# One order of steps for another: a delta-rule attention with a gated feed-forward, its hand-written step list rearranged

## The chip, the core and the metric

The kernel runs on one core of one Trainium2 chip. The time is the device time of one launch in microseconds, from start to end as the device counts it; three runs of the kernel before gave a median of 515.95 us. The change is called faster or slower by the ratio of such times.

## What is computed

The reference has two halves. The first walks 768 tokens one after another for 4 batches x 8 heads, with a 48 x 48 state for each; the second is a gated feed-forward on its output (`x`, 4 x 768 x 384).

```python
k_n = k / (norm(k) + 1e-06)
for t in range(768):                       # (b, h): 4 x 8 states of 48 x 48
    y[:, :, t] = q_t @ state
    v_old = k_t @ state
    state = state + beta_t * outer(k_t, v_t - v_old)
x = y.transpose(0, 2, 1, 3).reshape(4, 768, 384)

h = gelu(x @ w_in)                         # 384 -> 1024
u, v = h[..., :512], h[..., 512:]
v_n = layer_norm(v) * g_ln
v_s = einsum('ts,bsd->btd', w_sg, v_n) + b_sg[None, :, None]
out = x + (u * v_s) @ w_out
```

## The kernel before

**Chunks and segments.** The walk over tokens is cut into chunks. The program counts 12 chunks, 0 to 11: each holds 64 tokens of two batches at once (16 pairs of batch and head, of which half lies on partitions 0 to 63 and half on 64 to 127), and chunks 0 to 5 serve one pair of batches and 6 to 11 the other. Two chunks are a segment (0 to 5). Within a chunk the recurrence is solved with matrices: the products of the chunk's keys and queries (`gram`), the inverse of a unit triangular matrix of 64 x 64 for each pair (its blocks of 32 x 32 on VectorE in `lanes`, the rest by small matmuls), and then a chain of matmuls that carries the state.

**Steps.** A string, PROGRAM, lists some 800 steps by name. A loop at the end of the function calls each in turn, so the string sets the order of instructions on every engine and in every queue. A step reads `name:chunk` or `name:half:chunk`; a letter names the queue of a DMA (S is SyncE's, A is ScalarE's, P is GpSimd's). Those that matter here:

- `kd:c:x:q`, `kq:c:x:q`, `kt`, `v`: loads of a chunk's keys and queries (448 KB each piece), by the helper `load` (L172). `kd` feeds `gram`, `kq` the chain. There are two buffers of each, so chunk 9's `kd` needs `gram:7` to be over. Each load further waits for the latest copy that a chain step before it in the list has marked (`own`'s or `state`'s copy on ScalarE).
- `gram:c` (matmuls `ps<-kd`), copied by ScalarE to `gm`; `gstore:c` (L267) writes a part of `gm` to DRAM (`gd`), `zload:s` (L342) reads a whole segment back as `zl`, in a layout that has the matrices along the partitions.
- `lanes:0`, or `bglanes:g` and then `l:n`: the inverse on `zl`. `bglanes` puts its operations (one or two for each column of a block; 58 or more for a group) into a list and `l:n` issues the next n of them, most on VectorE; the first makes a copy on VectorE (L364) and two `affine_select` on GpSimd (L366). Groups are segments 0, 1, 2 with 3, and 4 with 5. Its end stores `zd` (L470).
- `blocks:c` and `heads:c` (L476): the stored inverse comes back as `z` and `zk`. They issue whatever is left of the segment's `l` operations first.
- `turned`, `join:0..3` (chunks 0 to 3), `corner_a`, `corner_b`: matmuls with a masked copy on VectorE between them (`j`, L504), which put the blocks of 64 x 64 together.
- `old:e:c`, `own:e:c`, `state:e:c` for e = 0, 1: the chain. `old`'s product is added to `v` on VectorE (L616), `own`'s is copied to `u` (L638), `state`'s to `s` and `x` (L651, L666) on ScalarE. `old:1` may carry a third argument, the chunk whose first quarter of `gram` it is mixed with.
- `turn:c` (L767), `gate:c:d` (L745 to L747), `values:c:n` (L781): the feed-forward's first layer for a chunk that is through the chain, in pieces. `ustore`, `xstore`, and a store within `values` go through SyncE's queue. `d:n` decodes a piece of `w_in` on VectorE and ScalarE, `w:k` loads one, `norms`, `mask`, `vprep` are small preparations.
- `kick`, `warm`: matmuls on zeros that nobody reads. `unit`, `late_weights`, `last_part`: decoding of the late weights.

What comes behind the list (the spatial product with `w_sg` and the last projection, 864 matmuls, "the tail" below) is ordered by the compiler and is the same in both kernels.

TensorE has one helper line, L115, for nearly all matmuls of the attention, so rows are told apart by their tiles: `ps<-kd` is `gram`, `ps<-j,ztk` is `join` or `corner_b`, `ps<-s,kq` is `old`, `ps<-v,z` is `own`.

Of the kernel before, what the change touches and what calls it, by code (L numbers as in the profile page):

```python
# [67 lines left out]
l:2 corner_a:6 kt:6:S turned:6 gate:4:1 gate:4:2 gate:4:3 own:1:5 l:1 vprep:6 corner_b:6 l:3 state:1:5 l:9 kq:7:0:S
turn:5 old:0:6 heads:7:P kt:7:P own:0:6 state:0:6 values:4:8 l:13 old:1:6 kq:7:1:S values:4:10 blocks:7:S gate:5:0
v:7:S vprep:7 values:5:16 ustore:4 gate:5:1 l:1 values:5:2 mask:10 l:1 turned:7 xstore:5 corner_a:7 l:2 own:1:6 l:1  # L70
state:1:6 turn:6 gate:5:2 gate:5:3 bgnorm l:2 ustore:5 old:0:7 values:6:5 corner_b:7 kq:8:1:P xstore:6 blocks:8:S:P
kq:8:0:A norms:4 v:8:A own:0:7 gate:6:0 heads:8:S:P values:6:4 state:0:7 old:1:7 vprep:8 own:1:7 gate:6:1 values:6:2
gate:6:2 turned:8 heads:9:A state:1:7 blocks:9:A corner_a:8 kt:8:P gate:6:3 values:6:1 l:8 v:9:P values:6:4 turned:9
corner_b:8 old:0:8 turn:7 own:0:8 kq:9:0:P state:0:8 ustore:6 corner_a:9 l:11 norms:5 l:7 old:1:8 vprep:9 xstore:7
l:11 values:6:2 own:1:8 gate:7:0 state:1:8 corner_b:9 heads:10:S:P late_weights kq:9:1:S unit:1 gate:7:1 values:7:5
mask:9 old:0:9 kt:9:S unit:1 v:10:P values:7:13 kq:10:0:S own:0:9 turn:8 gate:7:2 values:8:1 gate:7:3 kt:10:S unit:1
blocks:10:A ustore:7 state:0:9 gate:8:0 gate:8:1 unit:1 old:1:9 turned:10 unit:1 gate:8:2 own:1:9 gate:8:3 kq:10:1:A
kq:11:0:A unit:1 ustore:8 corner_a:10 mask:11 state:1:9 turn:9 heads:11:A vprep:10 values:8:10 old:0:10 gate:9:0
corner_b:10 unit:1 gate:9:1 blocks:11:S own:0:10 values:8:5 unit:1 v:11:A xstore:8 state:0:10 unit:1 gate:9:2
kq:11:1:P unit:1 values:8:2 values:9:5 unit:1 old:1:10 vprep:11 corner_a:11 values:9:2 unit:1 turned:11 own:1:10  # L80
unit:1 values:9:11 state:1:10 unit:1 kt:11:A gate:9:3 turn:10 corner_b:11 old:0:11 unit:1 ustore:9 unit:1 unit:1
gate:10:0 values:10:14 own:0:11 xstore:9 values:10:4 unit:1 state:0:11 gate:10:1 old:1:11 own:1:11 gate:10:2
# [1089 lines left out]
```

## Time and profile before

| | us |
|---|---|
| median of three runs | 515.95 (514.07 to 516.02) |
| the profiled execution | 512.55 |
| its span in the trace | 510.8 |
| TensorE busy | 452.8 (89% of the span) |
| VectorE busy | 332.4 (65%) |
| ScalarE busy | 171.8 (34%) |
| mean granted clock of TensorE | 0.92 |

The span is what the trace covers; the profiled execution took 1.75 us more than that, and the median run 3.40 us more than the profiled one. The chain of work that ended last is 74% TensorE, 13% DMA, 7% VectorE and 3% ScalarE. A granted clock of 1.00 is 2.4 GHz, one of 0.50 is 1.2 GHz.

### The profile page before, as it was taken

How to read it: one execution, taken by the hardware profiler on the slowest of the kernel's cores; microseconds unless marked ns; L12 is line 12 of the kernel's file. 1: busy time of each engine (PE TensorE's matmuls, PEld its weight loads, DVE VectorE, ACT ScalarE, POOL GpSimd, SP SyncE). 2: the span in 40 equal slices, each digit the busy share in tenths (PEclk: the TensorE clock that was granted, in tenths of full speed). 3: DMA queues.
4: the chain of work that ended last, by engine and by line, in shares of the span. 5: the costliest groups of instructions: out<-in, count | busy, mean ns of one | idle time of the engine just before them, and what ended most of it. 6: DMA issues, size and time to landing. Idle time of an engine off the chain costs nothing.

```text
span 510.8 us, 17402 instructions
## 1 busy us (share of the span) xinstructions
PE 452.8 (89%) x7563; PEld 414.5 (81%) x7563; DVE 332.4 (65%) x728; ACT 171.8 (34%) x403; POOL 92.7 (18%) x120
## 2 busy tenths in 40 slices
...
PEclk9875765795999997899999999999999999999999
...
GB/s 203 213 271 220 152 239 150 130 174 246 110 166 283 262 187 196 198 111 214 196 188 200 279 222 226 232 121 224 280 176 151 170 155 116 101 154 149 85 17 139
DMA packets 96557, 93.30 MB, mean 183 GB/s; under 512 B 55184, under 2 KB 71552, under 8 KB 96480
## 3 DMA queue, kind: packets, MB, share of 16 engines
...
q14 instruction: 18, 0.15, 0.1%
...
## 4 chain that ended last, share of the span: by engine, by line
PE 74%; DMA 13%; DVE 7%; ACT 3%; issue 2%; SPq 1%; POOL 0%; ACTq 0%; POOLq 0%; DVEq 0%
PE ps L115 23%; PE ps L745 14%; PE ps L747 13%; PE ps L746 13%; PE ps L781 9%; DMA gd<-gm 3%; DMA zl<-gd 3%; DMA kd<-kqT 3%; DMA kq<-kqT 2%; PE ps L767 1%; DVE ztmp L420 1%; DVE zl L427 1%; SPq L267 1%; DMA z<-zd 1%; DMA v<-vtok 1%
## 5 line engine op out<-in xcount | busy, mean ns | idle before, releaser
L888 POOL TENSOR_TENSOR ga<-ga,uT 128x384 f32<-128x384 f32 x32 | 35.7, 1118 | 144.5 <-DMA vraw<-vD 54.0
L115 PE MATMUL ps<-s,kq 48*64 48x48 f32 x1408 | 54.4, 228 | 4.6 <-ACT s L651 3.5
L115 PEld LDWEIGHTS ps<-s,kq 48*64 48x64 f32 x1408 | 48.2, 142 | 11.7 <-issue 4.9
L115 PE MATMUL ps<-kd 48*64 48x128 f32 (+1 forms) x768 | 33.4, 350 | 22.9 <-DMA kd<-kqT 19.3
L115 PEld LDWEIGHTS ps<-kd 48*64 48x64 f32 x768 | 30.3, 191 | 24.2 <-issue 16.4
L745 PE MATMUL ps<-xh,winh 128*128 128x256 f32 x144 | 43.6, 303 | 0.0
L750 ACT CAST gh<-ga 128x384 fp32r<-128x384 f32 x32 | 16.3, 511 | 75.1 <-POOL ga L888 69.5
L746 PE MATMUL ps<-xl,winh 128*128 128x256 f32 x144 | 40.6, 282 | 0.0
L747 PE MATMUL ps<-xh,winl 128*128 128x256 f32 x144 | 40.6, 282 | 0.0
L115 PE MATMUL ps<-z,gm 32*64 32x64 f32 x640 | 27.5, 248 | 12.2 <-DMA z<-zd 11.8
L751 DVE TENSOR_TENSOR gl<-ga,gh 128x384 fp32r<-128x384 f32 x32 | 18.5, 580 | 29.7 <-ACT gh L750 29.6
L420 DVE TENSOR_TENSOR ztmp<-zl 128x28 f32<-128x28 f32 (+20 forms) x84 | 36.0, 428 | 2.7
L427 DVE TENSOR_TENSOR zl<-zl,ztmp 128x28 f32<-128x28 f32 (+20 forms) x84 | 35.9, 427 | 2.4
L115 PEld LDWEIGHTS ps<-z,gm 32*64 32x64 f32 x640 | 24.6, 158 | 14.9 <-issue 12.4
L115 PE MATMUL ps<-v,z 64*64 64x48 f32 x768 | 31.6, 231 | 5.4 <-DVE v L616 3.0
L115 PEld LDWEIGHTS ps<-v,z 64*64 64x64 f32 x768 | 27.9, 146 | 7.4 <-DVE v L616 2.7
L745 PE MATMUL ps<-wsgh,vnh 128*128 128x384 f32 x96 | 32.6, 340 | 0.0
L745 PE MATMUL ps<-wsgh,winh 128*128 128x384 f32 x96 | 32.5, 339 | 0.0
L746 PE MATMUL ps<-wsgl,winh 128*128 128x384 f32 x96 | 32.5, 339 | 0.0
L747 PE MATMUL ps<-wsgh,winl 128*128 128x384 f32 x96 | 32.5, 339 | 0.0
L747 PE MATMUL ps<-wouth,gl 128*128 128x384 f32 x96 | 32.4, 339 | 0.0
L745 PE MATMUL ps<-wouth,gh 128*128 128x384 f32 x96 | 32.3, 339 | 0.0
(140 smaller groups left out, 1141.4 us busy)
## 6 DMA issues: line engine op xcount, KB each, us to landing
...
kd<-kqT ACTq DMA_DIRECT2D x9, 448.0 KB, 5.9
```

Of the source, the lines that this page charges most:

```text
L115: return nc.tensor.matmul(out=out, lhsT=lhsT, rhs=rhs, start=start, stop=stop, skip_group_check=True)
L267: queues[(half + sd) % len(queues)].dma_start(out=gdt[s][half, sd, c2].rearrange("j s t -> s j t"), in_=GK[c % N_M][r0:r0 + 32, half],)
L420: tv.tensor_tensor(out=products(i, r0, r1, at), in0=zb[:, :, r0:r1, i:i + 1].broadcast_to([P, nblk, r1 - r0, w]), in1=zb[:, :, i:i + 1, i ...
L427: tv.tensor_tensor(out=z_, in0=z_, in1=products(i, r0, r1, at), op=ALU.add)
L745: nc.tensor.matmul(out=ps, lhsT=sh, rhs=mh, start=(first and i == 0), stop=False)
L746: nc.tensor.matmul(out=ps, lhsT=sh, rhs=ml, start=False, stop=False)
L747: nc.tensor.matmul(out=ps, lhsT=sl, rhs=mh, start=False, stop=(last and i == n - 1))
L750: nc.scalar.copy(out=hi, in_=src)
L751: nc.vector.tensor_tensor(out=lo, in0=src, in1=hi.bitcast(F32), op=ALU.subtract)
L767: nc.tensor.transpose(out=ps[:, cc], in_=x[:, cc * P:(cc + 1) * P], identity=ident)
L781: nc.tensor.matmul(out=self.ps, lhsT=(self.xl if k == 2 else self.xh)[:, cc, bi], rhs=(winl if k == 1 else winh)[:, cc, DH:], start=(i == ...
L888: nc.gpsimd.tensor_tensor(out=gv, in0=gv, in1=uT[:, :, d], op=ALU.mult)
```

## The change

The list has the same steps in another order, and with other letters for the queues. No matmul is added or removed: the 4587 matmuls, the 858 VectorE and all ScalarE instructions of the two programs are the same in number and shape. What differs is where they stand, how `l` operations and `values` matmuls are split among the steps, and which queue issues a DMA: SyncE's has 293 instead of 303 of them, ScalarE's 39 instead of 54, GpSimd's 93 instead of 68.

The core of the diff is the list's opening and the two stretches that the prediction speaks of:

```diff
-keys:1:S keys:0:A consts beta:A kq:1:0:P kq:1:1:S kgram:0 kgram:1 kd:3:1:S gstore:0:S:A gstore:1:P kd:3:0:P kq:0:0:S
-kick:12 zload:0:A kd:2:1:A l:1 kd:2:0:A qgram:1 lanes:0 gram:3 kd:5:0:P gram:2 warm:9 kq:0:1:P w:0:A kt:0:P
-gstore:2:S:P kd:4:1:A v:0:S d:1 kd:4:0:A norms:0 d:1 gstore:3:S:A:P mask:3 qgram:0 blocks:0:S:P mask:0 d:1 zload:1:A
-join:0:0 heads:0:S bglanes:1 turned:0 join:1:0 vprep:0 l:1 join:2:0 join:3:0 mask:1 corner_a:0 kt:1:A blocks:1:S:P
-heads:1:P kd:5:1:S l:1 gram:5 old:0:0 gram:4 w:2:P v:1:S l:2 corner_b:0 kd:6:0:P l:28 join:0:1 kd:6:1:P kd:7:0:P l:2
+kick:12 beta:P keys:0:A keys:1:A kq:1:0:P consts kgram:0 kq:1:1:P kd:2:1:P gstore:0:S:P l:3 kgram:1 gstore:1:S:A:P
+zload:0:S kd:3:0:S w:0:S kd:3:1:P lanes:0 kd:2:0:A gram:3 norms:0 kd:5:0:P kq:0:1:A qgram:1 kq:0:0:P mask:3 l:5 gram:2
+qgram:0 mask:0 kd:4:0:S kd:4:1:P l:1 warm:9 gstore:2:S:P gstore:3:P blocks:0:A d:1 l:2 heads:0:S:A mask:1 v:0:S d:2
+zload:1:S join:0:0 turned:0 bglanes:1 kt:1:S v:1:S join:1:0 join:2:0 vprep:0 kd:5:1:A l:3 old:0:0 join:3:0 corner_a:0
+blocks:1:P l:6 corner_b:0 l:29 gram:4 gram:5 kt:0:P join:0:1 w:1:P vprep:1 kd:6:1:P kd:7:0:P kd:7:1:P heads:1:S:A
...
-own:1:1 mask:4 join:3:2 turn:0 mask:2 v:2:S corner_a:2 state:1:1 d:1 blocks:3:S:P turn:1 join:0:3 gstore:7:S:A:P
-corner_b:2 d:2 join:1:3 heads:3:S kd:9:0:A kd:8:0:P zload:2:P turned:3 zload:3:S bglanes:2 gram:8 v:3:S d:1 l:1
-kq:2:1:A kd:9:1:S l:2 vprep:2 xstore:1 old:0:2 gram:9 kt:2:A join:2:3 kq:3:0:S own:0:2 l:3 kq:3:1:A l:1 kd:10:1:S l:22
+v:2:A gstore:7:S:P heads:3:S:P join:3:2 corner_a:2 old:1:1:8 zload:2:P own:1:1 zload:3:P blocks:3:S d:3 kd:9:0:S
+state:1:1 mask:2 bglanes:2 kt:2:S kd:9:1:P gram:8 l:4 kq:2:1:P vprep:2 corner_b:2 l:8 join:0:3 turn:1 gstore:8:S:P
+turned:3 old:0:2 join:1:3 l:6 gram:9 kd:10:0:P v:3:P own:0:2 norms:3 gate:0:0 l:7 vprep:3 l:8 kd:11:1:P join:2:3
...
-gstore:8:S:P gstore:9:S:P kd:11:1:P kq:5:1:P state:1:3 gate:1:2 gate:1:3 v:5:P ustore:1 gate:2:0 gram:11 gate:2:1
-blocks:4:S:P l:5 xstore:2 heads:4:S:A:P gate:2:2 gate:2:3 turn:3 values:2:16 mask:7 kt:5:S corner_a:4 gram:10 turned:4
-gstore:10:S mask:6 old:0:4 zload:4:S vprep:5 mask:8 gate:3:0 values:2:1 heads:5:S:P corner_b:4 norms:3 gstore:11:S
-own:0:4 ustore:2 mask:5 gate:3:1 state:0:4 blocks:5:S:P zload:5:P kq:5:0:A gate:3:2 gate:3:3 old:1:4 values:2:1
-own:1:4 turned:5 state:1:4 bglanes:3 l:14 corner_a:5 xstore:4 old:0:5 xstore:3 l:4 corner_b:5 heads:6:P turn:4
+own:1:3 gate:1:3 xstore:2 gate:2:0 ustore:1 blocks:4:S v:5:A norms:2 mask:8 state:1:3 kq:5:1:P gate:2:1 heads:4:S:P
+gram:10 turn:3 mask:6 gstore:10:S:P gate:2:2 vprep:4 zload:4:S mask:7 values:2:4 gram:11 values:2:7 gstore:11:S:A
+vprep:5 old:0:4 gate:2:3 values:2:3 turned:4 corner_a:4 gate:3:0 heads:5:S mask:5 corner_b:4 l:7 mask:10 ustore:2
+zload:5:P gate:3:1 kq:5:0:P own:0:4 blocks:5:P gate:3:2 bglanes:3 turned:5 state:0:4 old:1:4 values:2:3 l:13
+values:2:1 heads:6:S:A:P own:1:4 gate:3:3 l:3 v:6:P state:1:4 corner_a:5 turn:4 blocks:6:S:P l:3 turned:6 l:3 old:0:5
...
```

Three places of it, as the engines' queues have them. In the rows, `kd_95`, `kq_107` and `z_105` are the buffers of odd chunks, `kd_94`, `kq_106` and `z_104` those of even ones, and `gm_96` to `gm_103` those of chunks 8 to 11 and 4 to 7.

SyncE's queue before, from the blocks of chunk 3 on:

```order
L476 DMA z_105<-zd 32x16x32 x2
L267 DMA gd<-gm_103 32x16x32
L476 DMA zk<-zd 64x8x32 x4
L342 DMA zl<-gd 128x1024
L172 DMA v_110<-vtok 128x2x384
L172 DMA kd_95<-kqT 112x2x512
L812 DMA xD_73<-x 128x2x384
L172 DMA kq_107<-kqT 112x2x512
```

and after:

```order
L267 DMA gd<-gm_103 32x16x32 x2
L476 DMA zk<-zd 64x8x32 x2
L476 DMA z_105<-zd 32x16x32 x4
L172 DMA kd_95<-kqT 112x2x512
L172 DMA kt_113<-ktok 128x2x384
L267 DMA gd<-gm_96 32x16x32 x2
L172 DMA kq_107<-kqT 112x2x512
L788 DMA vD_75<-vg 128x512
```

The reload of segment 3 (`zl`, `zload:3`) has left SyncE's queue, and a piece of chunk 9's keys (`kd_95`) stands right behind the blocks of chunk 3. GpSimd's queue at the same place, before:

```order
L476 DMA z_105<-zd 32x16x32 x2
L267 DMA gd<-gm_103 32x16x32
L172 DMA kd_94<-kqT 112x2x512
L342 DMA zl<-gd 128x1024
L366 AFFINE_SELECT zl<-zl 128x1024 x2
L172 DMA kt_114<-ktok 128x2x384
```

and after:

```order
L267 DMA gd<-gm_103 32x16x32 x2
L476 DMA zk<-zd 64x8x32 x2
L342 DMA zl<-gd 128x1024 x2
L172 DMA kd_95<-kqT 112x2x512
L366 AFFINE_SELECT zl<-zl 128x1024 x2
L172 DMA kq_106<-kqT 112x2x512
```

Both reloads of the pair of segments, the other piece of chunk 9's keys and, behind the two selects, a piece of chunk 2's `kq` now stand in this queue. SyncE's queue some 70 us later, at the stores of chunks 10 (`gm_98`) and 11 (`gm_99`), before:

```order
L267 DMA gd<-gm_98 32x16x32 x4
L342 DMA zl<-gd 128x1024
L476 DMA zk<-zd 64x8x32
L267 DMA gd<-gm_99 32x16x32 x4
L807 DMA uD_77<-ut 128x2x512
L476 DMA z_105<-zd 32x16x32 x2
```

and after:

```order
L267 DMA gd<-gm_98 32x16x32 x2
L342 DMA zl<-gd 128x1024
L788 DMA vD_75<-vg 128x512
L267 DMA gd<-gm_99 32x16x32 x2
L476 DMA zk<-zd 64x8x32 x2
L807 DMA uD_77<-ut 128x2x512
```

Half of each chunk's four stores have gone to other queues. The reload `zl` between them is `zload:4`; `zload:5` is in GpSimd's queue in both kernels.

## Rows read from the trace of the kernel before

**Rows 1.** The page: busy time by engine, and TensorE's granted clock in 40 slices.

```profile
PE 452.8 (89%) x7563; PEld 414.5 (81%) x7563; DVE 332.4 (65%) x728; ACT 171.8 (34%) x403; POOL 92.7 (18%) x120
PEclk9875765795999997899999999999999999999999
```

**Rows 2.** Stretches: start:end length, busy (count) of each engine, granted clock, DMA share, GB/s.

```profile
68.40:95.70 27.30, 25.92 (x563) 24.05 (x565) 22.45 (x46) 10.68 (x31) 5.62 (x8) 0.50 0.60 153
96.00:113.00 17.00, 14.28 (x514) 12.96 (x506) 12.98 (x23) 8.14 (x20) 3.22 (x5) 1.00 0.75 186
116.20:129.80 13.60, 6.25 (x164) 5.89 (x168) 11.28 (x27) 4.36 (x15) 2.50 (x2) 0.50 0.73 233
198.10:208.30 10.20, 5.56 (x103) 4.97 (x104) 9.59 (x25) 2.23 (x5) 2.70 (x4) 0.50 0.38 88
209.00:350.00 141.00, 135.01 (x2861) 116.72 (x2860) 98.40 (x231) 58.34 (x136) 9.59 (x14) 1.00 0.69 201
354.00:510.00 156.00, 153.22 (x868) 152.71 (x867) 80.60 (x149) 34.08 (x60) 35.71 (x32) 1.00 0.48 145
```

**Rows 3.** Chain that ended last, 107 to 131 us: start, length, what.

```profile
107.42 6.39 DMA gd<-gm
113.93 0.35 SPq L342
114.37 0.40 SPq L172
114.82 8.49 DMA kd<-kqT
123.55 6.85 PE ps L115 x192
```

**Rows 4.** TensorE's timeline, 110 to 129 us; in brackets the idle time before.

```profile
110.84 1.98 PE L115 MATMUL ps<-kd 48*64 48x128 f32 x64
123.55 3.69 PE L115 MATMUL ps<-kd 48*64 48x128 f32 x64 [9.82 <-DMA kd<-kqT]
127.17 1.74 PE L115 MATMUL ps<-j,ztk 64*32 64x32 f32 x64
```

**Rows 5.** DMA issues of 0 to 140 us: queue, count, size, median us to landing.

```profile
kd<-kqT ACTq DMA_DIRECT2D x8, 448.0 KB, 5.9
kd<-kqT POOLq DMA_DIRECT2D x6, 448.0 KB, 4.6
kd<-kqT SPq DMA_DIRECT2D x5, 448.0 KB, 5.8
kq<-kqT POOLq DMA_DIRECT2D x2, 448.0 KB, 5.8
```

**Rows 6.** GpSimd's timeline, 117 us: the selects of `lanes`.

```profile
117.95 2.50 POOL L366 TENSOR_SCALAR_AFFINE_SELECT zl<-zl 128x1024 f32<-128x1024 f32 x2 [9.98 <-DVE d L364]
```

**Rows 7.** The stretch 100 to 150 us, columns as in rows 2.

```profile
100.00:150.00 50.00, 36.38 (x1037) 32.20 (x1037) 45.66 (x87) 18.38 (x44) 9.07 (x12) 0.86 0.63 176
```

**Rows 8.** Chain that ended last, 181 to 203 us.

```profile
181.60 1.10 SPq L267
...
186.77 3.89 DMA gd<-gm
...
191.42 5.23 DMA zl<-gd
...
202.08 0.61 DVE j L504
202.74 1.92 PE ps L115 x32
```

**Rows 9.** Chain that ended last, 36 to 69 us, at the opening's end.

```profile
36.24 0.34 SPq L470
...
46.26 5.56 DMA zl<-gd
...
63.49 0.60 DVE j L504
```

More of the change, by code (lines that the diff above doesn't have):

```diff
@@ L53 @@
-join:1:1 turned:1 own:0:0 l:2 vprep:1 gstore:4:S:A:P w:1:A state:0:0 kd:7:1:A old:1:0:6 own:1:0 join:2:1 blocks:2:P
-norms:1 d:4 l:4 join:3:1 gstore:5:S:A heads:2:S:A d:1 state:1:0 corner_a:1 gram:6 xstore:0 join:0:2 d:1 corner_b:1 l:3
-old:0:1 gstore:6:S:A:P d:2 kd:8:1:A own:0:1 turned:2 join:1:2 d:2 gram:7 join:2:2 state:0:1 kq:2:0:S old:1:1 d:1
-own:1:1 mask:4 join:3:2 turn:0 mask:2 v:2:S corner_a:2 state:1:1 d:1 blocks:3:S:P turn:1 join:0:3 gstore:7:S:A:P
-corner_b:2 d:2 join:1:3 heads:3:S kd:9:0:A kd:8:0:P zload:2:P turned:3 zload:3:S bglanes:2 gram:8 v:3:S d:1 l:1
@@ L58 @@
-kq:2:1:A kd:9:1:S l:2 vprep:2 xstore:1 old:0:2 gram:9 kt:2:A join:2:3 kq:3:0:S own:0:2 l:3 kq:3:1:A l:1 kd:10:1:S l:22
-l:3 vprep:3 values:0:6 join:3:3 state:0:2 old:1:2 gate:0:0 own:1:2 l:12 kt:3:P corner_a:3 state:1:2 old:0:3 l:10
-gate:0:1 kq:4:1:A values:0:12 corner_b:3 own:0:3 values:1:1 kq:4:0:S state:0:3 gate:0:2 gate:0:3 norms:2 l:2 old:1:3
-l:6 turn:2 v:4:S kt:4:S vprep:4 l:2 kd:11:0:A own:1:3 l:1 ustore:0 gate:1:0 values:1:17 gate:1:1 kd:10:0:S
-gstore:8:S:P gstore:9:S:P kd:11:1:P kq:5:1:P state:1:3 gate:1:2 gate:1:3 v:5:P ustore:1 gate:2:0 gram:11 gate:2:1
@@ L63 @@
-blocks:4:S:P l:5 xstore:2 heads:4:S:A:P gate:2:2 gate:2:3 turn:3 values:2:16 mask:7 kt:5:S corner_a:4 gram:10 turned:4
-gstore:10:S mask:6 old:0:4 zload:4:S vprep:5 mask:8 gate:3:0 values:2:1 heads:5:S:P corner_b:4 norms:3 gstore:11:S
-own:0:4 ustore:2 mask:5 gate:3:1 state:0:4 blocks:5:S:P zload:5:P kq:5:0:A gate:3:2 gate:3:3 old:1:4 values:2:1
-own:1:4 turned:5 state:1:4 bglanes:3 l:14 corner_a:5 xstore:4 old:0:5 xstore:3 l:4 corner_b:5 heads:6:P turn:4
-kq:6:0:A l:3 own:0:5 blocks:6:S v:6:S values:3:4 l:6 state:0:5 gate:4:0 l:3 ustore:3 l:1 values:3:14 kq:6:1:P old:1:5
@@ L68 @@
[L68 to L82, printed above, removed]
@@ new lines @@
+zload:1:S join:0:0 turned:0 bglanes:1 kt:1:S v:1:S join:1:0 join:2:0 vprep:0 kd:5:1:A l:3 old:0:0 join:3:0 corner_a:0
+blocks:1:P l:6 corner_b:0 l:29 gram:4 gram:5 kt:0:P join:0:1 w:1:P vprep:1 kd:6:1:P kd:7:0:P kd:7:1:P heads:1:S:A
+kd:6:0:P own:0:0 w:2:A gstore:4:A join:1:1 state:0:0 turned:1 old:1:0 join:2:1 own:1:0 blocks:2:P d:4 join:3:1
+heads:2:A state:1:0 gram:6 l:3 corner_a:1 mask:4 d:1 norms:1 gstore:6:S l:1 d:1 kd:8:0:P join:0:2 d:1 xstore:0
+corner_b:1 kd:8:1:P kq:2:0:P old:0:1 gstore:5:S:A:P join:1:2 d:1 gram:7 turned:2 own:0:1 d:4 state:0:1 turn:0 join:2:2
@@ new lines @@
+v:2:A gstore:7:S:P heads:3:S:P join:3:2 corner_a:2 old:1:1:8 zload:2:P own:1:1 zload:3:P blocks:3:S d:3 kd:9:0:S
+state:1:1 mask:2 bglanes:2 kt:2:S kd:9:1:P gram:8 l:4 kq:2:1:P vprep:2 corner_b:2 l:8 join:0:3 turn:1 gstore:8:S:P
+turned:3 old:0:2 join:1:3 l:6 gram:9 kd:10:0:P v:3:P own:0:2 norms:3 gate:0:0 l:7 vprep:3 l:8 kd:11:1:P join:2:3
+state:0:2 old:1:2 kq:3:1:S kt:3:P join:3:3 l:5 values:0:11 kq:3:0:S kd:11:0:S own:1:2 l:5 state:1:2 corner_a:3
+gate:0:1 kt:4:P values:0:6 gstore:9:S l:9 old:0:3 v:4:S xstore:1 l:4 corner_b:3 gate:0:2 kq:4:1:S values:0:1 gate:0:3
@@ new lines @@
+kq:4:0:P values:1:12 own:0:3 l:5 values:1:6 ustore:0 state:0:3 gate:1:0 old:1:3 turn:2 kd:10:1:A gate:1:1 l:2 gate:1:2
+own:1:3 gate:1:3 xstore:2 gate:2:0 ustore:1 blocks:4:S v:5:A norms:2 mask:8 state:1:3 kq:5:1:P gate:2:1 heads:4:S:P
+gram:10 turn:3 mask:6 gstore:10:S:P gate:2:2 vprep:4 zload:4:S mask:7 values:2:4 gram:11 values:2:7 gstore:11:S:A
+vprep:5 old:0:4 gate:2:3 values:2:3 turned:4 corner_a:4 gate:3:0 heads:5:S mask:5 corner_b:4 l:7 mask:10 ustore:2
+zload:5:P gate:3:1 kq:5:0:P own:0:4 blocks:5:P gate:3:2 bglanes:3 turned:5 state:0:4 old:1:4 values:2:3 l:13
@@ new lines @@
+values:2:1 heads:6:S:A:P own:1:4 gate:3:3 l:3 v:6:P state:1:4 corner_a:5 turn:4 blocks:6:S:P l:3 turned:6 l:3 old:0:5
+l:3 xstore:3 l:4 corner_b:5 l:1 kq:6:0:P values:3:11 kq:6:1:A gate:4:0 kt:5:P own:0:5 xstore:4 l:5 ustore:3 values:3:7
+l:1 gate:4:1 state:0:5 heads:7:A corner_a:6 vprep:6 kt:6:P old:1:5 l:1 values:4:16 l:1 own:1:5 l:6 values:4:2
+corner_b:6 kq:7:0:P state:1:5 old:0:6 l:4 own:0:6 l:1 gate:4:2 turned:7 v:7:P turn:5 gate:4:3 blocks:7:S:P kt:7:A
+state:0:6 l:5 old:1:6 l:3 corner_a:7 gate:5:0 ustore:4 l:5 vprep:7 kq:7:1:S values:5:18 own:1:6 l:1 kq:8:1:P norms:4
@@ new lines @@
+v:8:S gate:5:1 state:1:6 corner_b:7 xstore:5 turn:6 old:0:7 xstore:6 gate:5:2 gate:5:3 own:0:7 ustore:5 values:6:1
+blocks:8:S gate:6:0 values:6:2 state:0:7 values:6:4 vprep:8 gate:6:1 kq:8:0:P values:6:3 old:1:7 heads:8:P gate:6:2
+kt:8:S own:1:7 values:6:1 turned:8 heads:9:S:P gate:6:3 state:1:7 values:6:7 blocks:9:P corner_a:8 old:0:8 corner_b:8
+turn:7 own:0:8 state:0:8 norms:5 values:7:2 gate:7:0 bgnorm old:1:8 values:7:1 xstore:7 kq:9:0:P ustore:6 kt:9:P
+corner_a:9 kq:9:1:A l:1 v:9:S turned:9 l:3 mask:9 l:2 late_weights own:1:8 l:1 heads:10:S vprep:9 blocks:10:S:A:P
```

11 lines of the change are left out of this document (9 added, 2 removed).

## The prediction

> **What bounds the kernel now.** I read the busy times first, then stretches, then the chain that ended last. TensorE is busy for 452.8 of 510.8 us [rows 1], so an order of steps can only win back the 58 us in which TensorE stands still, and the time that it works at half clock. Where both lie is plain from the clock row [rows 1]: the low slices are in the first quarter and one more near 200 us; from there it is at full clock to the end. The stretch 209 to 350 us has 135.01 busy of 141.00 us, and the tail 153.22 of 156.00 [rows 2]. The tail is not in the list, so it stays; between 209 and 350 us there are 6 us to lose or win in all. What a new order can move is ahead of 209 us, and there I find two places where TensorE waits for a transfer that a queue held back.
>
> Place A is the longest wait of the middle. `gram:9` starts at 123.55 after 9.82 us of idleness, waiting for `kd` [rows 4]. The chain tells why [rows 3]: stores of `gm` to DRAM land at 113.8 (107.42 + 6.39), only then does SyncE issue `zload:3` (L342, 113.93), then `v`, and at 114.82 the `kd` piece of chunk 9, which takes 8.49 us. The piece did not need `zload:3`; it stood behind it in SyncE's queue. After the wait the granted clock is 0.50 from 116.20 to 129.80 [rows 2]: `gram:9` takes 3.69 us where `gram:8` took 1.98, and `join:2` 1.74 us [rows 4].
>
> Place B is smaller. `corner_b:5` starts at 202.74, when VectorE has made `j` at 202.08 + 0.61 [rows 8]. Back along the chain: SyncE issues the eight stores of chunks 10 and 11 in turn from 181.60, the last lands at 190.7 (186.77 + 3.89), `zload:5` is issued at 191.42 and lands at 196.65, and the first 14 operations of `lanes:3` stand on VectorE ahead of the `j` that TensorE wants. The idle time, from `corner_a:5`'s end, is 4.86 us; behind it the clock is 0.50 from 198.10 to 208.30 [rows 2], and `corner_b` takes 1.92 us.
>
> **The opening.** `kick` stands first, the keys come on one queue, `zload:0` goes from ScalarE's queue to SyncE's. By the instructions ahead of them I expect `lanes:0` to end some 2 us earlier than the store at 36.24 [rows 9], and `zload:1` to be issued near 40 instead of 46.26, since SyncE's queue has less ahead of it. That does not reach the chain: in the new order 38 `l` operations stand on VectorE ahead of `join:0:1`'s masked copy, not 32, so that copy, at 63.49 before [rows 9], comes at about 62. Against it, `corner_b:0` now precedes two grams, and ScalarE issues six DMAs between the copies of `own:0:0` and `state:0:0`, at some 0.35 us each by the queue rows of SyncE [rows 3, 9]: 1 to 2 us. Net 0, with 3 us either way for what I can't see.
>
> **68 to 96 us.** The same matmuls, at half clock before [rows 2], and I expect the same clock, as TensorE comes out of the same long waits of the opening. Four decode steps (`d:4`) now put a cast ahead of `state:0:1`'s copy on ScalarE: chunk 1's chain ends some 2.7 us later, by the VectorE work that leads to this cast. This delay starts place A and is counted there.
>
> **Place A.** One piece of chunk 9's `kd` stands in SyncE's queue behind the blocks of chunk 3, the other in GpSimd's behind `zload:2` and `zload:3`. Both need `gram:7` and the marked copy, so I put their issue at 108 to 109, and they land 5.8 us (SyncE) and 4.6 us (GpSimd) later [rows 5], at 114 to 115; I allow 118 for a full DMA. `gram:9` follows at about 116.7, when the banks that VectorE frees allow it, against 123.55. Next in line is a piece of `kq` for chunk 2: it is behind the two selects of `lanes:2`, which take 2.50 us and wait for `zload:3` [rows 6]. So it is issued near 114 and lands at 120 (5.8 us, [rows 5]). Then `own:0:2` ends at about 122, not at 130.40, where the chain's stretch after the wait ends [rows 3]; but `join:2:3` (1.26 us at full clock) was before it and now is behind. That is 8.4 - 1.3 = 7.1 us. What is late next is VectorE: it was busy 45.66 of the 50 us from 100 to 150 [rows 7], so only 4.3 us of idleness are there to be taken out, and the rest must come from work that moves behind. Adding up its instructions from 100 us to `old:1:3` in the new order gives 51 us, so with the start 2.7 us later that step comes about where it was, or 1 us earlier; but by then TensorE has 17 `values` matmuls and a gate more behind it (17 x 0.235 + 1.25 = 5.2 us, both from the trace's own values and gates). I take 5 us as the gain. The bounds: 9.82 + 2.6 (half clock: 1.7 for the gram, 0.5 for the join, 0.4 for `own`) = 12.4 us, of which nothing is lost; and -1, where VectorE idles for a `kq` landing two transfers later.
>
> **Place B.** In the new order `gram:10` and `gram:11` come close together, with the stores shared among SyncE, GpSimd and ScalarE, and `zload:5` needs after `gram:11`: copies and issue 2.6 us, landing 3.89, issue 0.5, landing 5.23 [rows 8], 12.2 us; VectorE's operations up to `j` add 5.4 (196.65 to 202.08, [rows 8]). Against 17.6 us stand, from `gram:11` to `corner_a:5`, 14 values (3.3), five gates (6.3), two corners (2.2), and two each of `old`, `own` and `state` (6.9): 18.7 us of TensorE work, and `corner_a:5` itself 1.1. So the wait goes, with 2 us in hand, and with it the half clock behind it: 4.86 + 2.0 (`corner_b` 0.8, `turn` 0.7, `old` and `own` the rest) = 6.9, I take 7. If the landing takes 5 us more, 3 of it come back; the bounds are 2 and 7.
>
> By the row, the new queues cost nothing for themselves: a `kd` piece lands in 4.6 us from GpSimd's queue, in 5.8 from SyncE's and 5.9 from ScalarE's [rows 5]. The Trainium skill speaks against this part of the change: "DMA: Bandwidth & Descriptors", section "Issuing engine by pattern", gives simple loads to Sync and calls the hardware path generally faster, and its "Specifications" put a first byte of the GpSimd path at about 1 us against 0.6. By it each of 25 transfers moved to GpSimd would be 0.4 us later, an estimate of 10 us if all were waited for, and of 1 to 2 us for the three or four that are; the rows show the opposite sign for the same piece.
>
> **The rest.** From 209 us on TensorE has work at nearly all times in the old order, and I see no large wait in the new one: a `kq` of chunk 3 behind a `values` store (1 us), `kq:11:0` issued 6.4 us of TensorE work ahead of its use, against 5.8 us of landing. I take 1 us off. Sum: 0 + 5 + 7 - 1 = 11 us.
>
> **Rivals.** *The half clock lasts.* The stretch 68.40 to 95.70 is at 0.50 and 96 to 113 at 1.00 [rows 2]. If with the new order the low clock went on to `gram:8`, the 14.28 us of work in the second stretch would take longer by between 1.74/1.26 and 3.69/1.98 [rows 4], about 1.6 times: +8.6 us, leaving 2.4 of 11: 513.5. For it: the order ahead of 96 us is altered in every place. Against it: TensorE has as much work there as before. *GpSimd's queue becomes the block.* `zload:3` now precedes `kd` and `kq` in that queue, as it preceded `kd` in SyncE's. If chunk 7's stores are as late as before (113.93, [rows 3]), `kd` lands at 119, `zload:3` at 118 to 119, the selects end at 121.5, `kq` lands at 127.3, `own:0:2` ends at 131.4 and `join:2:3` is still to come: 2.3 us behind the old order instead of 7 ahead, and `lanes:2` ends 4 to 7 us later than before, which holds the blocks of chunk 4. That is 8 us lost: 524. It decides from about 111.7 on for the issue of `zload:3`. For it: the stores of chunk 7 took 6.39 us [rows 3]. Against it: `gram:7` and its stores stand earlier, I expect the issue at 100 to 106. *No half clock at 68 to 96.* The opening's waits are shorter by a few us; if the clock is 1.00 there, the 25.92 us of work [rows 2] shrink by up to 12 us: 493.
>
> **How the numbers follow.** The profiled execution of 512.55 less 11 is 501.5; the median of before lies 3.4 higher, and I carry that: 505.0. Of the forecast the chance is 0.55, its own range 500 to 510 by the bounds of A and B; the lasting half clock 0.14, GpSimd's block 0.16, the full clock 0.15. The range runs from 493, the full clock's time, to 517, past the lasting half clock's, and leaves out the block. What a measurement can tell from no change is 0.5%, 2.6 us: 513.4 to 518.5. Faster: 0.55 + 0.15 = 0.70; same 0.14; slower 0.16.
>
> **What would show it.** Right: `gram:9` starts before 118 with no wait of over 3 us for `kd`, the waits for `kd` and for `j` ahead of `corner_b:5` are gone from TensorE's list, the granted clock is 1.00 from 100 us to the end, and the tail starts some 11 us earlier. Wrong: TensorE waits for `kq` at `own:0:2` beyond 124, or VectorE has idle time between 100 and 150 us together with TensorE, or a wait of some us appears behind 209 us.

## The result, and the profile after

The changed kernel takes 509.11 us (median of ten runs), the kernel before 514.53 us in the same comparison: a ratio of 0.987 with a 95% interval of 0.983 to 0.991. That is 6.6 us faster, by the interval 4.5 to 8.7, where the forecast was 11 us. The medians alone differ by 5.4 us; the ratio leaves out the runs that lie over 1.5% above the fastest of their kernel, four of the ten of the changed kernel among them.

The page of the changed kernel, the lines that answer to [rows 1]; the profiled execution is 508.10 us long, its span 506.0:

```profile
PE 451.6 (89%) x7562; PEld 412.1 (81%) x7563; DVE 331.5 (66%) x728; ACT 171.9 (34%) x403; POOL 111.1 (22%) x145
PEclk9566587759999999999999999999999999999999
```

TensorE is as busy as before, and the slice near 200 us that was at a lower clock is gone. But the low slices at the front have not become fewer: they are the 2nd to the 9th now. Stretches of the changed kernel, columns as in [rows 2]:

```profile
62.00:112.00 50.00, 40.72 (x1191) 37.83 (x1189) 40.63 (x85) 20.27 (x59) 14.18 (x21) 0.74 0.81 199
100.00:150.00 50.00, 43.01 (x1092) 38.38 (x1093) 45.61 (x89) 21.86 (x57) 11.55 (x16) 0.90 0.80 213
198.00:346.00 148.00, 142.02 (x2956) 123.89 (x2955) 102.68 (x244) 62.73 (x145) 16.23 (x24) 0.99 0.72 205
346.00:506.00 160.00, 154.36 (x868) 152.44 (x866) 82.05 (x150) 34.47 (x57) 37.38 (x32) 1.00 0.44 139
```

In the 50 us from 100 on, TensorE works 43.0 instead of 36.4 us [rows 7], and VectorE, with 45.6, as much as before. The tail has 154.4 busy of 160 us from its start to the end of the span.

TensorE's waits by what released them, 40 to 353 us, the kernel before first (total, times, longest):

```profile
PE ps L115 <- DMA z<-zd: 11.8, 3, 10.6
PE ps L115 <- DMA kd<-kqT: 9.8, 1, 9.8
PE ps L115 <- DVE j L504: 4.9, 1, 4.9
PE ps L115 <- ACT s L651: 3.5, 5, 1.1
```

and the changed kernel, 40 to 350 us:

```profile
PE ps L115 <- issue: 11.3, 10, 1.6
PE ps L115 <- DMA z<-zd: 7.3, 4, 5.6
PE ps L115 <- ACT s L651: 4.6, 4, 3.1
PE ps L115 <- ACT u L638: 2.8, 4, 0.9
PE ps L115 <- DVE j L504: 2.1, 2, 1.3
```

The 9.8 us for `kd` are gone here, the 4.9 us for `j` have become 1.3, and a 3.1 us wait for ScalarE's copy to `s` is new. Most of the first line is new as well: "issue" is idle time for which the profile names nothing that TensorE waited for. The kernel before has 0.9 us of it, in two places. Every profile used below of a kernel with the new list's middle shows 5.8 to 12.7 us of it, the others 2.2 to 3.7. No run takes it apart, so its cause stays open.

To see where time is won and lost along the list, I subtract from the end of a step the work done by then: the sum of the full-clock durations of all steps of TensorE up to it (`gram` 1.98, `own` 1.15, a `values` matmul 0.235 and so on, from the traces). What is left is time lost to idleness and half clock. It is worked out from the two traces, in us:

| end of step | before: at / lost | after: at / lost | lead |
|---|---|---|---|
| `join:0:1` | 61.5 / 39.3 | 65.0 / 42.8 | -3.4 |
| `state:1:1` | 105.5 / 54.4 | 112.2 / 61.1 | -6.7 |
| `own:0:2` | 130.4 / 67.7 | 123.9 / 62.4 | 5.3 |
| `state:1:3` | 163.9 / 69.4 | 163.5 / 65.0 | 4.4 |
| `state:1:5` | 223.6 / 76.7 | 218.4 / 69.8 | 7.0 |
| `state:1:7` | 263.5 / 80.0 | 253.6 / 68.9 | 11.1 |
| start of the tail | 354.3 / 81.0 | 346.3 / 73.0 | 8.0 |
| end of the tail | 507.2 | 502.4 | 4.8 |

So the lead is 11 us at `state:1:7`; 3 us of it go behind that, and 3.2 in a tail that is longer (156.2 us instead of 152.9). And ahead of place A the new list is 6.7 us behind.

Each column is one execution, though, and two of the kernels below, front_new and tail_units, have the same list as the changed kernel up to `state:1:3`. Their `join:0:1` ends at 61.9 and 63.6 (65.0 here), their `state:1:1` at 108.2 and 112.0 (112.2 here). The granted clock differs as well, though the list is the same; 84 to 93 us in the changed kernel and in tail_units:

```profile
84.00:93.00 9.00, 7.65 (x225) 6.86 (x221) 7.97 (x14) 3.94 (x13) 2.90 (x5) 1.00 0.83 184
84.00:93.00 9.00, 8.90 (x149) 8.19 (x153) 8.83 (x16) 3.83 (x12) 3.42 (x5) 0.50 0.87 208
```

So a lead or a time taken from one profile is uncertain by some 4 us in this part of the program, and what a part of the list costs is better taken from the times below.

### The profile page after: what moved, and what is told of

Same layout as the page of the kernel before. It is cut to its first block, busy times and chain, and to the rows that moved or that the text cites. A ratio compares the mean times of both kernels' runs of the same rounds, so it can differ in the third digit from the quotient of the medians.

```text
span 506.0 us, 17425 instructions
## 1 busy us (share of the span) xinstructions
PE 451.6 (89%) x7562; PEld 412.1 (81%) x7563; DVE 331.5 (66%) x728; ACT 171.9 (34%) x403; POOL 111.1 (22%) x145
## 4 chain that ended last, share of the span: by engine, by line
PE 58%; DVE 19%; DMA 12%; issue 4%; SPq 2%; ACT 2%; ACTq 1%; DVEq 0%
PE ps L115 19%; PE ps L745 10%; PE ps L747 10%; PE ps L746 10%; PE ps L781 7%; DVE zl L427 4%; DVE ztmp L420 4%; DMA kd<-kqT 3%; DMA vraw<-vD 2%; DMA zl<-gd 2%; DMA uT<-uD 2%; DMA gd<-gm 2%; DMA zd<-zl 1%; PE ps L767 1%; DVE zl L396 1%
## 5 line engine op out<-in xcount | busy, mean ns | idle before, releaser
L888 POOL TENSOR_TENSOR ga<-ga,uT 128x384 f32<-128x384 f32 x32 | 37.4, 1173 | 139.2 <-DVE rsq_t L203 51.8
L115 PE MATMUL ps<-kd 48*64 48x128 f32 (+1 forms) x768 | 30.2, 317 | 14.7 <-DMA kd<-kqT 14.7
L115 PEld LDWEIGHTS ps<-kd 48*64 48x64 f32 x768 | 27.3, 168 | 16.4 <-issue 14.5
L115 PE MATMUL ps<-u,gm 64*64 64x48 f32 x768 | 30.7, 234 | 2.4 <-ACT u L638 1.3
```

The source lines that it names most:

```text
L115: return nc.tensor.matmul(out=out, lhsT=lhsT, rhs=rhs, start=start, stop=stop, skip_group_check=True)
L888: nc.gpsimd.tensor_tensor(out=gv, in0=gv, in1=uT[:, :, d], op=ALU.mult)
```

## The experiments

Several kernels below join the two lists: one list up to a named step, then all steps that are left, in the other list's order. All of them compute the same thing. Ratios are to the kernel before, measured beside it.

**a_swap: the `kd` piece alone.** In the list before:

```diff
-... zload:2:P turned:3 zload:3:S bglanes:2 gram:8 v:3:S d:1 l:1 kq:2:1:A kd:9:1:S l:2 ...
+... zload:2:P turned:3 kd:9:1:S zload:3:S bglanes:2 gram:8 v:3:S d:1 l:1 kq:2:1:A l:2 ...
```

> The kernel before, with one step moved: kd:9:1 stands ahead of zload:3 in SyncE's queue. If place A is what the prediction says, gram:9 starts at 116 to 119 instead of 123.55, and the tail starts 4 to 7 us earlier than at 354.30 (ratio to before 0.986 to 0.992). If VectorE, busy for 45.7 of 50 us there, takes it back, gram:9 starts as early, but the tail starts within 2 us of 354.30 (ratio 0.996 to 1.000).

Ratio 1.015 (1.007 to 1.023): slower. `gram:9` starts at 117.65, within the forecast, and `own:0:2` ends at 128.3, 2.1 us earlier than before; the loss comes behind that. TensorE's and VectorE's timelines of a_swap, with the waits that matter:

```profile
117.65 2.96 PE L115 MATMUL ps<-kd 48*64 48x128 f32 x64 [2.29 <-DMA kd<-kqT]
126.29 0.34 PE L115 MATMUL ps<-s,kq 48*64 48x48 f32 x2 [4.12 <-DVE v L616]
139.97 0.34 PE L115 MATMUL ps<-v,z 64*64 64x48 f32 x2 [3.28 <-DVE v L616]
...
122.00 0.22 DVE L364 COPY d<-zl 128x64 f32<-128x64 f32 x1 [6.16 <-DMA zl<-gd]
125.68 0.55 DVE L616 TENSOR_TENSOR v<-v,ps 128x384 f32<-128x384 f32 x1
```

Behind the `kd` piece `zload:3` goes out at 116.84 instead of 113.93. VectorE's next instruction is the first of `lanes:2`, which needs it; VectorE stands still for 6.2 us, and the addition to `v` that `own:0:2` waits for stands behind that instruction. In the kernel before that copy came at 117.66, after 1.6 us. TensorE then waits a second time for an addition to `v`, ahead of `own:1:2`, which ends at 141.9 instead of 137.9, and from 140 to 150 us it is at half clock, where the kernel before had 1.00:

```profile
140.00:150.00 10.00, 9.04 (x195) 8.58 (x196) 9.07 (x16) 1.34 (x3) 3.36 (x5) 0.50 0.32 69
```

At `state:1:3` a_swap is 8.4 us behind (172.3, 163.9 before). So the piece alone was not what held place A: `zload:3` and VectorE were right behind it, and neither of the two expectations (a gain, or a gain taken back) allowed for a loss. That VectorE's wait for `zload:3` is what makes the second addition late follows from the order of its queue in this one profile.

**a_store7: `zload:3` earlier.** In the list before:

```diff
-... join:0:3 gstore:7:S:A:P ...
+... join:0:3 gstore:7:S:P ...
```

> The kernel before with one step's queues changed: gstore:7 on SyncE and GpSimd instead of SyncE, ScalarE and GpSimd; its last store was issued at 107.4 from ScalarE's queue, and zload:3 waited for it until 113.93. Theory: place A is held by zload:3, for which VectorE waits with the v of old:0:2 queued behind, and VectorE is full. Then zload:3 goes out by 110, VectorE no longer idles at 116, gram:9 starts at 116 to 120, and the tail starts 1 to 3 us earlier than 354.30 (ratio 0.993 to 0.998). Rival, the prediction's own words (the kd piece is what TensorE lacks): the tail starts 4 to 7 us earlier (ratio 0.986 to 0.992).

Ratio 0.996 (0.992 to 1.001). SyncE's and VectorE's timelines of a_store7:

```profile
110.12 0.43 SPq L342 DMA_DIRECT2D zl<-gd  x1
111.10 0.60 SPq L172 DMA_DIRECT2D kd<-kqT  x1
...
117.95 0.21 DVE L364 COPY d<-zl 128x64 f32<-128x64 f32 x1
```

`zload:3` goes out 3.8 us earlier, VectorE doesn't wait for it, and the tail starts at 350.51, 3.8 us earlier in this profile, between the two expectations (1 to 3, and 4 to 7). By the times the gain is about 2 us and not clear of zero, so the run leans to VectorE's limit and does not rule the rival out. `gram:9` starts at 121.67 and not at 116 to 120: the `kd` piece was issued 3.7 us earlier than before but took 10.3 us to land, not 8.5. Part of place A is thus the landing itself; in the changed kernel the two pieces took 4.4 and 5.4 us. Four loads of this size are in flight at once there in the kernel before; whether they slow each other, no run separates.

**front_new: the new list up to `state:1:3`, then the old one.**

> The new list up to state:1:3, then the old list's rest: the new opening and place A, without B. In the changed kernel state:1:3 is 4.4 us of TensorE work-time ahead of before. If the parts add up, the wait ahead of corner_b:5 is back at 4 to 5 us and the tail starts 3 to 5.5 us earlier than 354.30 (ratio 0.989 to 0.994). If the lead of the front only holds with the new list behind it, the tail starts within 2 us of 354.30.

Ratio 1.002 (0.997 to 1.006): nothing is left. `state:1:3` has a lead of 5.1 us by the measure above; `own:0:4` has 1.4, and `corner_b:5` waits for `j` again. So the rival's expectation came true: the first half of the new list, by itself, gains nothing.

**mid_new: the old list up to `join:0:1`, the new one up to `state:1:3`, then the old one.** This is front_new without the new opening.

> The old list up to join:0:1, the new list up to state:1:3, then the old list's rest: place A with what leads to it, without the new opening and without B. b_long, with B alone, gave 0.988; open_old, with both and the new ending, 0.978. If A and B add, this gives 0.987 to 0.992, and state:1:3 ends with 6.5 to 8 us of TensorE work-time ahead of before. If the lead of A is lost again in the old list behind it (front_new gave 1.002, with the new opening), TensorE waits 3 us or more ahead of own:0:4 and the ratio is 0.995 to 1.002.

Ratio 0.994 (0.989 to 0.998), 3.3 us, 1.2 to 5.4 by the interval, between the two expectations; beside front_new it puts the new opening at 0.008 (0.002 to 0.014), some 4 us of loss. Its lead at `state:1:3` is 4.0 us, less than expected, and its chain that ended last shows why the old list can't use it all, 164 to 175 us:

```profile
164.99 0.47 DVE zl L409 x2
165.62 1.24 DVE zl L395
166.90 4.34 DMA zd<-zl
171.71 3.48 DMA z<-zd
```

`lanes:2` ends on VectorE at 166.9, the store and reload take until 175.2, and TensorE, ahead of time, waits for `z`. VectorE is ahead too, but by less: the store of `lanes:2` went out at 169.83 before. TensorE's wait is 1.5 us, and behind it the granted clock is 0.56 from 176 to 182 us, where it was 1.00 before:

```profile
175.23 1.14 PE L114 MATMUL ps<-z,gm 32*64 32x64 f32 x30 [1.49 <-DMA z<-zd]
```

**b_stretch and b_long: place B alone.** Old list up to `state:1:3`, new list up to `state:1:5` (b_stretch) or `state:1:7` (b_long), old list.

> The kernel before up to state:1:3, then the steps of the new list up to its state:1:5, then the old list's rest: place B alone, with the old opening and the old place A. If place B's wait is the stores' queue, the wait for j ahead of corner_b:5 falls from 4.86 us to under 1.5, and the tail starts 4 to 7 us earlier than 354.30 (ratio 0.986 to 0.992). If the wait only moves behind, corner_b:5 starts without it and the tail starts within 2 us of 354.30.

> The kernel before up to state:1:3, the new list up to state:1:7, then the old list's rest; the l operations are counted by what they pop, so that 17 are left for blocks:8 as in the new list (in b_stretch 23 were, by the way that it was put together, and TensorE waited 3.9 us there for VectorE). Theory: place B's gain holds where VectorE's lanes:3 is spread as in the new list: no wait above 2 us between corner_b:5 and state:1:7, and the tail starts 5 to 8 us earlier than 354.30 (ratio 0.984 to 0.990). Rival: VectorE's lanes:3 ends no earlier than at 253.9 as in b_stretch, and the tail starts within 2 us of 354.30.

b_stretch: 1.004 (1.000 to 1.008), though place B itself is mended: `corner_b:5` ends at 199.43 instead of 204.66, and `state:1:6` has a lead of 6.6 us. It was all lost at `own:1:7`, which ran from 251.07 to 257.15 with a wait of 3.9 us for VectorE: 23 operations of `lanes:3` were left for `blocks:8` there, which took VectorE from 242.07 to 253.90. The 23 come from the seam between the two lists. b_long, with the new list's spread and 17 left, and its order up to `state:1:7`: 0.988 (0.983 to 0.993), a gain of 6.0 us. So place B and what follows it up to `state:1:7`, some 100 us of the program, carry as much as the whole change. Of b_long only the times are used.

**open_old: the old list up to `join:0:1`, then the new one.**

> The old list up to join:0:1, then the new list's rest. The changed kernel ends join:0:1 at 64.97 where the kernel before ends it at 61.54. If the parts add up, all behind it comes 3 us earlier: state:1:1 ends at 108 to 109.5 (112.17) and the tail starts at 342.5 to 344 (ratio to before 0.979 to 0.983). If what comes behind (VectorE, ScalarE's issues of gstore:4) sets the pace to 112 us, state:1:1 ends at 111 to 112.5 and the tail starts at 345.5 to 346.5 (ratio 0.985 to 0.989).

Ratio 0.978 (0.969 to 0.986), median 503.05: faster than the kernel before, and than the changed kernel by a difference only just clear of zero (0.010, 0.001 to 0.019). `state:1:1` ends at 107.44 and the tail starts at 342.02. By this the new opening costs about 5 us. Over all runs: the three kernels with the old opening and the new rest (open_old, open_g4, open_g4_tail) have 0.978, 0.983 and 0.980, the three with the new opening (the changed kernel, act_free, tail_units) 0.987, 0.988 and 0.988, some 4 us apart.

Where the 4 us go the profiles do not show. mid_new has open_old's list up to `state:1:3`, and its `state:1:1` ends at 112.7, as late as in the changed kernel. So the 6.7 us of the table cannot all be put to the opening. At `join:0:1` the four old openings end at 60.4 to 62.7, the three new ones that keep the list as it stands at 61.9 to 65.0.

**act_free: what in the opening costs it.** In the changed list:

```diff
-... blocks:0:A ... gstore:4:A ...
+... blocks:0:S:P ... gstore:4:S:P ...
```

> The changed kernel with two letters changed: blocks:0 and gstore:4 go through SyncE's and GpSimd's queues, not ScalarE's. In the changed kernel ScalarE needs 3.9 us to issue the four loads of blocks:0 and 4.1 us for the four stores of gstore:4, where the prediction put some 0.35 us on each issue. If these issues are what the opening loses, join:0:0 starts at 42 to 43.5 (44.63), TensorE's 3.1 us wait for the copy to s at 71.3 is under 1 us, and the tail starts at 341 to 344 (346.25; ratio to before 0.974 to 0.981). If the opening's loss is VectorE's six more l operations ahead of join:0:1, and VectorE paces what follows, join:0:1 still ends after 63.5 and the ratio is 0.984 to 0.989.

Ratio 0.988 (0.981 to 0.994): no better than the changed kernel, the rival's value. The signs of the theory up to `join:0:1` came true all the same. ScalarE's timeline in the changed kernel, and the wait on TensorE that follows:

```profile
40.02 3.93 ACTq L476 DMA_DIRECT2D z<-zd  x4
...
66.60 4.12 ACTq L267 DMA_DIRECT2D gd<-gm  x4
70.75 0.48 ACT L651 COPY s<-ps 112x384 f32<-112x384 f32 x1 [4.19 <-issue]
...
71.29 1.14 PE L115 MATMUL ps<-s,kq 48*64 48x48 f32 x32 [3.09 <-ACT s L651]
```

The second row is four stores back to back, of 0.43, 0.59, 0.80 and 2.17 us. The first is four loads whose issues take 0.32, 0.76, 0.31 and 0.31 us, 1.70 in all; the rest of its 3.93 us are waits between them, so the 3.9 us of the expectation are not the price of issues. In act_free `join:0:1` ends at 62.77 (64.97) and the wait for `s` is 0.5 us. But `state:1:0` ends at 80.75, where it ended at 80.99. What has come in its place, TensorE and VectorE in act_free:

```profile
71.21 1.07 PE L115 MATMUL ps<-j,ztk 64*32 64x32 f32 x32 [3.58 <-DVE ztk L501]
74.38 1.07 PE L115 MATMUL ps<-j,ztk 64*32 64x32 f32 x32 [2.10 <-DVE ztk L501]
...
61.94 0.59 ACTq L476 DMA_DIRECT2D zk<-zd  x1
62.70 0.58 ACTq L476 DMA_DIRECT2D zk<-zd  x1
...
70.62 0.45 DVE L501 STREAM_TRANSPOSE ztk<-zk 128x256 f32<-128x256 f32 x1 [3.40 <-DMA zk<-zd]
73.79 0.45 DVE L501 STREAM_TRANSPOSE ztk<-zk 128x256 f32<-128x256 f32 x1 [2.73 <-DMA zk<-zd]
```

The new opening loads `heads:1` (`zk`) behind `join:0:1`, at about 62, and these loads take 8.6 to 11.1 us to land among the others; `turned:1` waits for them, and `join:2:1` for `turned:1`. The old opening issues them from GpSimd's queue at 53.63, and in open_old the same transposes run at 65.83 without a wait. In the changed kernel this second wait is not seen; it would have been hidden by the first. This is one profile of each: in front_new and tail_units, with the changed kernel's list, `state:1:0` ends at 77.9 and 78.7. That the later `heads:1` costs as much as the issues is therefore the reading that this profile offers, and not shown.

**open_g4: `gstore:4` off ScalarE, with the old opening.**

> open_old with gstore:4 on SyncE's and GpSimd's queues instead of ScalarE's. In open_old TensorE waits 3.0 us for the copy to s behind these stores. If the wait is on the path, state:1:1 ends at 103 to 105.5 (107.44) and the ratio to before is 0.970 to 0.975 (0.9776 in open_old). If VectorE paces this stretch, state:1:1 ends within 1 us of 107.4 and the ratio is 0.975 to 0.980.

Ratio 0.983 (0.976 to 0.991), not better than open_old; `state:1:1` ends at 110.97, not earlier, which neither expectation had. The copy to `s` is not late any more (2.0 us of waits for `s` in four places), and the time is unchanged within what can be measured. These stores stand behind `join:0:1` in both openings (open_old waits 3.0 us behind them, mid_new 2.7), so they cannot be what parts the two.

**tail_units, open_g4_tail, end_old: the tail.** In the changed list, and the same in open_g4's:

```diff
-... last_part values:11:2 unit:1 values:11:1 ... gate:11:3 unit:1 ustore:11 unit:1 unit:1
+... last_part values:11:2 unit:1 unit:1 unit:1 values:11:1 ... gate:11:3 unit:1 ustore:11
```

> The changed kernel, with two of the last units (pieces of v for the tail) taken from the list's very end to right behind last_part. The tail is 3.2 us longer in the changed kernel than before (346.25 to 502.41 against 354.30 to 507.22). If it waits for v pieces that are fetched too late, its waits of 2.0 us go and it is 153 to 154.5 us long, 1.5 to 3 us off the time of the changed kernel (ratio to before 0.981 to 0.984). If ScalarE then stands waiting for those pieces ahead of the last gates, the tail starts 1 to 3 us later and the time is that of the changed kernel (0.987).

> open_g4 with the two units moved as in tail_units. There the tail was 152.8 us long instead of 156.2, but the time was not measurably better than the changed kernel's. If the tail's length counts, this is 2.5 to 3.5 us faster than open_g4 (ratio to before lower by 0.005 to 0.007). If it is given back ahead of the tail, the two are within 1 us.

> The new list up to state:1:7, then the old list's rest. In the changed kernel 4.1 us are lost between state:1:7 and the tail (1.0 before), and its tail is 3.2 us longer. If both belong to the new list's ending, the tail starts at 342 to 344 (346.25 in the changed kernel) and is 152.5 to 153.5 us long: 5 to 7 us off the changed kernel's time (ratio to before 0.972 to 0.978). If the old ending can't take up the lead of 11 us, because its loads or VectorE come too late for it, waits of 3 us or more appear behind state:1:7 and the ratio is 0.983 to 0.988.

tail_units: the tail is 152.8 us long, as expected, and its profiled span is 2.9 us shorter than the changed kernel's; the ratio is 0.988 (0.981 to 0.995), the changed kernel's own within the interval. open_g4_tail: 0.980 (0.971 to 0.990) beside 0.983 for open_g4; its tail is 152.8 us too, but started 3.2 us later in the profile. The other kernels with the new ending as it stands have tails of 153.7 to 154.0 us, so of the 3.2 us by which the changed kernel's tail is longer about 1 belongs to the list and the rest to that execution. The loss between `state:1:7` and the tail is in all six that have the new ending, 3.0 to 5.3 us, against 0.7 at most in the three with the old one whose profiles are used. end_old, new list up to `state:1:7` and then the old one: 0.986 (0.976 to 0.995), where 0.972 to 0.978 had been expected of two losses in the new ending; the rival's value. The three intervals are 7 to 10 us wide, so that the ending costs or gains up to 3 us stays open.

## Why the prediction was right in its direction, and 4 us off in its size

**The sum and its range.** The time that was measured lies inside the range, and the change is faster, as forecast. The forecast's own range of 500 to 510, though, does not follow from the bounds that it names: with 2 to 7 for place B, -1 to 12.4 for place A and 1 us off they give 0 to 18.4 us of gain, about 497.5 to 516. So it is luck that 509.11 lies within 500 to 510, by 0.9 us.

**The two waits.** Both are where the profile showed them, and both are gone or small in the changed kernel. These are its rows at the two places, TensorE's timeline:

```profile
119.66 2.39 PE L115 MATMUL ps<-kd 48*64 48x128 f32 x64
122.60 0.32 PE L115 MATMUL ps<-s,kq 48*64 48x48 f32 x4 [0.55 <-DMA kq<-kqT]
...
192.08 1.27 PE L115 MATMUL ps<-z,gm 32*64 32x64 f32 x32 [1.02 <-DMA z<-zd]
196.51 1.08 PE L115 MATMUL ps<-j,ztk 64*32 64x64 f32 x32 [1.29 <-DVE j L504]
```

Beside [rows 4] and [rows 8]: `gram:9` has no wait ahead of it and `own:0:2` half a microsecond for `kq`, 4.86 us have become 1.29 ahead of `corner_b:5`, which ends at full clock in 1.08 instead of 1.92 us.

**Place A: the size roughly right, the cause half right.** The prediction took the gain as 5 us, because VectorE is next and because 17 `values` matmuls and a gate come ahead of it. Measured by itself it is 3.3 us (mid_new, 1.2 to 5.4); open_old against b_long gives about 5.5 with place B behind it, within 5 us either way and with the new ending in it. But it named the `kd` piece behind `zload:3` as what TensorE lacked. a_swap shows that taking it out of that queue position alone makes the kernel slower: the reload behind it is what VectorE waits for. In the changed kernel `zload:3` itself goes out early, at 105.66 instead of 113.93, from GpSimd's queue, and the `kd` pieces land faster (4.4 and 5.4 us). a_store7, with the early `zload:3` alone, has 2 us that are not clear of zero:

```profile
105.66 0.54 POOL L342 DMA_DIRECT2D zl<-gd  x1 [3.56 <-DMA gd<-gm]
113.37 0.70 POOL L172 DMA_DIRECT2D kd<-kqT  x1 [7.17 <-ACT s L651]
114.33 2.50 POOL L366 TENSOR_SCALAR_AFFINE_SELECT zl<-zl 128x1024 f32<-128x1024 f32 x2 [0.26 <-DVE d L364]
116.77 0.70 POOL L172 DMA_DIRECT2D kq<-kqT  x1
```

That issue time also decides the rival of GpSimd's queue, which needed 111.7 or later; it was forecast for 100 to 106. The issue of `kd`, forecast for 108 to 109, is 113.37, since `state:1:1` is 6.7 us late; nothing waited for it.

**Place B: right.** Forecast 7 us, measured 6.0 us (3.5 to 8.5) in b_long. In the changed kernel `zload:5` goes out at 184.02, 7.4 us earlier than in [rows 8]:

```profile
184.02 0.57 POOL L342 DMA_DIRECT2D zl<-gd  x1 [9.17 <-DVE ztk L501]
```

Whether that is the work of the stores shared among the queues or of the grams of chunks 10 and 11, the later of which now starts at 169.45 instead of 178.04, no run separates. b_stretch adds what the prediction did not say: the gain is lost again when VectorE has too much of `lanes:3` left at `blocks:8`. b_long differs from it in the order up to `state:1:7` too, so that the spread alone makes up for it is read from the wait in b_stretch, not measured by itself.

**The opening: the term that was mis-sized.** It stood at 0 with 3 us either way. It is a loss of about 4 us: 0.008 (0.002 to 0.014) from front_new against mid_new, 0.010 (0.001 to 0.019) from the changed kernel against open_old. With it the terms come to -4.5 + 3.3 + 6.0 = 4.8 us for parts measured alone, each known to 2 to 4 us, and 6.6 us measured together. The forecast's own steps for it, SyncE's and VectorE's timelines of the changed kernel:

```profile
35.22 0.35 SPq L470 DMA_DIRECT2D zd<-zl  x1
46.11 0.34 SPq L342 DMA_DIRECT2D zl<-gd  x1
...
65.85 0.68 DVE L504 TENSOR_TENSOR j<-ps,same_upper 128x512 f32<-128x512 f32 x1
```

`lanes:0` ends 1.0 us earlier than in [rows 9], not 2. `zload:1` was to go out near 40 and goes out at 46.11, as late as before. What SyncE waited for last is a load of `zk` that it had issued at 40.82 and that landed at 45.90, by its queue's waits from 41 to 47 us:

```profile
SPq L342 <- DMA zk<-zd: 2.9, 1, 2.9
```

In front_new, with the same opening, it goes out at 43.16. And `join:0:1`'s masked copy, with 38 `l` operations ahead of it as counted, comes at 65.85 instead of 62. The price of an issue on ScalarE was wrong as well: 0.35 us each, from single rows of SyncE's queue, where on ScalarE four loads took 1.70 us and four stores 4.12; the first row of [rows 8] already reads 1.10 us for one such store. But act_free, which takes these issues away, is no faster. The move of `heads:1` was not priced at all; in act_free's profile it costs as much again. What the 4 us consist of stays open: six `l` operations more, the later `heads:1`, the later `zload:1` and the low clock are all in the same stretch, and no run holds one of them fixed.

**The rest.** One microsecond had been taken off. Between `state:1:7` and the tail 3.1 us of the lead go, and the tail, which the prediction held fixed, is 3.2 us longer in this profile, about 1 in the others. Neither could be settled by the times (end_old, tail_units). TensorE's 11.3 us of "issue" had no term.

**The rival of the lasting half clock.** It had a chance of 0.14, and its sign is there: from 93 to 114 us the changed kernel (second row) has 0.59 where the kernel before (first row) had 0.94, and `gram:8` takes 2.92 us, not 1.98.

```profile
93.00:114.00 21.00, 18.00 (x601) 16.23 (x596) 16.88 (x30) 9.95 (x25) 3.93 (x6) 0.94 0.63 154
93.00:114.00 21.00, 17.49 (x466) 16.30 (x470) 18.00 (x33) 8.48 (x24) 5.67 (x9) 0.59 0.88 226
```

But it did not come on top: 84 to 93 us is at 1.00 in this profile, at 0.50 before, and from 62 to 130 us the clock is 0.80, against 0.70 before. The low clock has moved more than lasted. That the clock would be the same from 68 to 96 us, and full from 100 us on, was wrong; the step to 1.00 comes near 114 us.

**The signs that it named.** Of those for "right", the waits for `kd` and `j` came out as said. `gram:9` starts at 119.66, not before 118, and the tail starts 8.0 us earlier, not 11. Of those for "wrong" none came: the wait for `kq` at `own:0:2` is 0.55 us, at 122.60, and no wait behind 209 us is longer than 1.6.

The rule that the prediction set beside the queue rows had GpSimd's path slower. In the kernel before the rows had the opposite order [rows 5]. The changed kernel's, 0 to 140 us:

```profile
kd<-kqT POOLq DMA_DIRECT2D x13, 448.0 KB, 5.5
kd<-kqT ACTq DMA_DIRECT2D x4, 448.0 KB, 4.9
kd<-kqT SPq DMA_DIRECT2D x4, 448.0 KB, 4.9
```

With 13 of the 21 pieces in GpSimd's queue, that queue is the slowest, by 0.6 us. "DMA: Bandwidth & Descriptors" of the Trainium skill, section "Specifications", states about 1 against 0.6 us to the first byte; the order of these rows agrees with it, that of [rows 5] does not, and the pieces stand at other places in the two kernels, so no run sets the paths side by side. None of TensorE's long waits in the changed kernel past 40 us is for a `kd` piece, so it costs nothing here.
